# Issuing all loads, bit copies and stores from SyncE's queue, with the whole instruction order laid anew, in a bucketed-attention and MLP kernel

## The chip, the cores and the metric

The kernel runs on one core of a Trainium2 chip. The metric is the device time of one execution in microseconds (us); lower is better. The time before is the median of three runs.

## The reference, cut to what matters

Batch B = 4, H = 8 heads, S = 768 positions, D = 64; the MLP has 512 channels and 2048 hidden units. Each query and key gets six sign bits from a projection; a query attends only to keys whose six bits are all the same as its own.

```python
q_bits = (np.einsum('bhsd,dk->bhsk', q, proj) > 0)
k_bits = (np.einsum('bhsd,dk->bhsk', k, proj) > 0)
mask   = q_bucket[:, :, :, None] == k_bucket[:, :, None, :]   # buckets: the bits as a number
scores = np.where(mask, 0.125 * q @ k.T, -1e9)
attn   = softmax(scores)                                      # sum + 1e-9 below
x      = (attn @ v), the heads side by side: [4, 768, 512]
xn     = (x - mean) / sqrt(var + 1e-6) * g_ln
out    = x + relu(xn @ w_ch1) @ w_ch2
```

## The kernel before, in words

**The order.** The program is a list of 1138 words (ORDER, lines 19 to 117), and the loop at line 561 turns each word into the instructions of one small function. A word reads `name.engine.arguments`; the engine letter is v (VectorE, DVE), a (ScalarE, ACT), p (GpSimd, POOL), s (SyncE, SP) or t (TensorE, PE). Every engine executes its own words strictly in the order of the list, and so does the queue from which it issues DMAs: a DMA word that has to wait holds back everything behind it on its engine. The order and the engine letters were found by annealing against a planner's costs. The semaphores and waits are put in by the framework. It gives each DMA that SP or ACT issues one of eight shared semaphores (99, 101, 103, 105, 106, 107, 108 and 110 in the trace), in turn over both queues together, and a DMA waits, before it is issued, until the last DMA on the same semaphore has landed, whichever queue that one came from.

**The attention.** The work is cut into 12 units u, each 256 queries of one batch (batch b has units 3b to 3b+2), times two groups g of four heads, times three blocks kp of 256 keys: 72 score blocks s = 6u + 3g + kp.

- `LX` (line 393; `lx`, 289, in pieces for batch 0) loads q or k of one batch and head group, 768 KB, into one of four X buffers; `tu` and `tn` turn it in 32 by 32 squares on DVE; `CA` and `ca` (`cast`, 247 to 253) cast it to bf16.
- `hm` (403; `hc` for batch 0) projects it, and `bt` (416) turns the signs into bits. `mo` (419) copies these bits, 4.5 KB at a time, to the partitions where the score matmuls read them, the tile G. That is 16 small SBUF to SBUF DMAs for each batch and head group, 96 in all: the arguments of `mo.b.g.c.i` are batch, group, key quarter c (192 columns) and head i.
- `lv` (354) loads v into one of two buffers, `cv` (360) casts it and `su` (366 to 373, three adds) sums it, both on POOL; `sp` and `sc` spread that sum.
- `S` (432, matmuls at 444) makes a score block from the bits and from q and k, `E` (449) is its exponential on ACT, two halves for each block, `A` (452, 459) multiplies by v and adds up in PSUM.

**The MLP.** `na` (470), `nb` (476; the multiply of 481 reads two SBUF operands), `nc` (483) and `ce` (487; 489 reads two SBUF tensors) divide by the row sum and normalize on DVE, and `rs` (493) makes the inverse deviation on POOL. `fl` (497) transposes xn by a DMA, which only SP issues. `F` (511, matmuls at 516) is a pair of hidden tiles, and `R` (521) its relu, on DVE (526) or ACT (524). F has a single PSUM buffer, f1, so the next F waits for the last R. `D` (528, 532) is a quarter of the second product, `Z` (539) adds the residual on DVE, `O` (545) stores 128 KB of x, which is one of four x buffers.

SP issues 155 DMAs before the change: 7 lx, 15 lv, 10 LX, 71 mo, 22 fl, 30 O. ACT issues 66: the projection, 11 lv, 2 LX, the load of g_ln (`lg`), 25 mo, 26 O. POOL issues the 8 weight loads. ACT's DMA words stand between its exponentials and relus; line 42 of the list begins with `mo.a.1.0.2.1`, and line 68 with `lv.a.3.4.0`.

Of the kernel before, what the change touches and what calls it, by code (L numbers as in the profile page):

```python
# [19 lines left out]
lp.a mem.v p32.p warm.t lx.s.0.0.0.1 tn.v.0.0.0 hc.t.0.0.0 ca.v.0.0.0 bc.v.0.0.0 lx.s.0.1.1.3 tn.v.0.1.2 sel.p  # L20
sl.t.0.0.0 bi.a.0.0.0 on.p.0 hc.t.0.1.2 lx.s.1.0.0.1 bc.v.0.1.2 ca.p.0.1.2 pmem.p sl.t.0.1.2 tn.v.0.1.1 hc.t.0.1.1
tn.v.1.0.0 lx.s.0.1.0.1 bc.v.0.1.1 lx.s.1.1.0.3 ca.p.0.1.1 lv.a.0.0.4 bi.a.0.1.2 S.t.2.2 lx.s.0.0.1.3 tn.v.0.1.0
E.a.2.0 hc.t.1.0.0 lv.s.0.4.4 sl.t.0.1.1 bc.v.1.0.0 sl.t.1.0.0 bi.v.1.0.0 bi.a.0.1.1 tn.v.1.1.1 ca.p.0.1.0 ca.p.1.1.1
hc.t.0.1.0 E.a.2.1 S.t.1.2 bc.v.0.1.0 sl.t.0.1.0 lw1.p.1 tn.v.1.1.0 bi.v.0.1.0 lw1.p.3 hc.t.1.1.0 bc.v.1.1.0
ca.v.1.0.0 hc.t.1.1.1 bc.v.1.1.1 E.a.1.0 cv.p.0.0.0 S.t.0.2 E.a.1.1 E.a.0.0 tn.v.1.1.2 ca.p.1.1.2 cv.p.0.0.2
lx.s.1.0.1.3 E.a.0.1 sl.t.1.1.0 bi.v.1.1.0 sl.t.1.1.1 bi.v.1.1.1 LX.s.1.0.1 hc.t.1.1.2 S.t.4.2 tn.v.0.0.2 E.a.4.0
E.a.4.1 tn.v.0.0.1 hc.t.0.0.1 A.t.0.2 bc.v.1.1.2 lv.s.1.0.0 ca.v.1.1.0 sl.t.1.1.2 bi.a.1.1.2 S.t.3.2 ca.p.0.0.1
tn.v.1.0.2 A.t.1.2 bc.v.0.0.1 cv.p.0.4.0 A.t.2.2 E.a.3.0 tn.v.1.0.1 ca.v.1.0.1 E.a.3.1 sl.t.0.0.1 bi.v.0.0.1
tu.v.1.0.1.2 lg.a sq.t.0.0 sc.a.0.0 S.t.5.2 tu.v.1.0.1.1 E.a.5.0 E.a.5.1 na.v.0.0 hc.t.1.0.2 bc.v.1.0.2 lw1.p.2
ca.v.0.0.2 lw2.p.0 cv.p.0.4.2 sq.t.0.4 sc.a.0.4 lw1.p.0 sl.t.1.0.2 tu.v.1.0.1.0 S.t.8.2 E.a.8.0 E.a.8.1 hc.t.1.0.1  # L30
lv.a.1.0.3 bc.v.1.0.1 A.t.5.2 sl.t.1.0.1 nb.v.0.0 A.t.4.2 A.t.3.2 bi.v.1.0.2 tu.v.1.0.1.3 S.t.6.2 E.a.6.0 na.v.0.1
bi.v.1.0.1 E.a.6.1 hc.t.0.0.2 nc.v.0.0 bc.v.0.0.2 sl.t.0.0.2 LX.s.1.0.0 bi.a.0.0.2 tu.v.1.0.0.3 S.t.7.2 lv.s.1.0.1
nb.v.0.1 nc.v.0.1 E.a.7.0 E.a.7.1 A.t.6.2 A.t.8.2 ce.v.0.0 ft.t.0.0 ce.v.0.1 ft.t.0.1 S.t.9.2 E.a.9.0 E.a.9.1
fc.v.0.1 A.t.7.2 fc.v.0.0 F.t.0.6 R.v.0.6 F.t.0.7 R.a.0.7 S.t.10.2 na.v.1.0 tu.v.1.0.0.0 rs.p.0 F.t.0.2 E.a.10.0
F.t.0.5 lv.s.1.4.0 E.a.10.1 LX.a.1.1.0 R.a.0.2 A.t.9.2 R.v.0.5 tu.v.1.0.0.1 S.t.11.2 E.a.11.0 A.t.10.2 F.t.0.3
tu.v.1.0.0.2 CA.v.1.0.0 F.t.0.4 E.a.11.1 nb.v.1.0 R.a.0.4 S.t.14.2 A.t.11.2 E.a.14.0 R.v.0.3 E.a.14.1 lw2.p.1 F.t.0.0
R.a.0.0 F.t.0.1 lv.s.1.0.2 S.t.12.2 nc.v.1.0 hm.t.1.0 R.a.0.1 na.v.1.1 nb.v.1.1 nc.v.1.1 ce.v.1.0 LX.s.1.1.1 on.p.1
fl.s.1.0 E.a.12.0 ce.v.1.1 bt.v.1.0 D.t.0.0.0 lv.s.1.4.1 fl.s.1.1 E.a.12.1 ca.v.1.0.2 lw2.p.2 S.t.13.2 CA.v.1.0.1
mo.s.1.0.2.0 tu.v.1.1.0.1 tu.v.1.1.1.1 mo.s.1.0.1.3 tu.v.1.1.0.2 tu.v.1.1.0.3 tu.v.1.1.1.0 su.p.1.0 D.t.0.0.1
D.t.0.0.2 tu.v.1.1.0.0 LX.s.2.0.0 E.a.13.0 mo.s.1.0.2.2 A.t.12.2 E.a.13.1 A.t.13.2 S.t.16.2 tu.v.1.1.1.2 tu.v.1.1.1.3  # L40
hm.t.1.1 CA.v.1.1.1 bt.v.1.1 lw2.p.3 lv.s.1.4.2 mo.s.1.0.3.3 D.t.0.0.3 mo.s.1.1.3.3 mo.s.1.0.3.2 lv.a.1.4.3
mo.a.1.0.2.1 Z.v.0.0 E.a.16.1 mo.s.1.0.1.2 F.t.1.2 E.a.16.0 su.p.1.4 A.t.14.2 na.v.2.0 mo.s.1.0.0.1 rs.p.1
mo.a.1.0.0.0 mo.a.1.1.1.0 mo.s.1.1.0.0 S.t.15.2 tu.v.2.0.0.0 R.a.1.2 F.t.1.0 LX.s.2.1.0 D.t.0.1.0 mo.s.1.0.0.3
mo.a.1.1.2.0 cv.p.1.4.0 mo.s.1.0.1.0 tu.v.2.0.0.2 cv.p.1.4.2 mo.s.1.0.3.0 E.a.15.1 mo.s.1.0.2.3 D.t.0.1.1 E.a.15.0
mo.a.1.0.1.1 R.v.1.0 F.t.1.1 S.t.17.2 mo.a.1.0.0.2 nb.v.2.0 nc.v.2.0 R.a.1.1 D.t.0.1.2 F.t.1.5 mo.s.1.1.1.1 E.a.17.0
mo.s.1.0.3.1 R.v.1.5 LX.s.2.0.1 D.t.0.1.3 E.a.17.1 cv.p.1.0.0 mo.s.1.1.0.3 S.t.18.2 E.a.18.0 F.t.1.4 CA.v.1.1.0
A.t.15.2 mo.s.1.1.1.3 Z.v.0.1 R.v.1.4 lv.a.2.0.2 A.t.17.2 A.t.16.2 na.v.2.1 F.t.1.3 lv.s.2.0.1 tu.v.2.0.0.1 E.a.18.1
cv.p.1.0.2 O.s.0.1 lv.a.2.4.3 S.t.20.2 mo.a.1.1.1.2 nb.v.2.1 nc.v.2.1 mo.s.1.1.0.2 ce.v.2.1 D.t.1.0.0 R.a.1.3 F.t.1.6
E.a.20.1 E.a.20.0 D.t.1.0.1 R.v.1.6 S.t.19.2 ce.v.2.0 mo.s.1.1.3.1 mo.a.1.1.0.1 E.a.19.0 F.t.1.7 tu.v.2.0.0.3
D.t.1.0.2 mo.a.1.1.2.1 R.v.1.7 D.t.1.0.3 Z.v.1.0 sp.t.1.0 E.a.19.1 A.t.20.2 sc.a.1.0 S.t.21.2 sp.t.1.4 mo.s.1.1.2.2  # L50
mo.a.1.1.3.2 D.t.1.1.0 E.a.21.0 A.t.18.2 tu.v.2.0.1.0 E.a.21.1 mo.s.1.1.2.3 fl.s.2.1 sc.v.1.4 fl.s.2.0 F.t.2.4
R.v.2.4 rs.p.2 lv.s.2.4.2 S.t.22.2 E.a.22.0 A.t.19.2 E.a.22.1 F.t.2.0 na.v.3.0 tu.v.2.0.1.1 R.a.2.0 D.t.1.1.1
mo.s.1.1.3.0 S.t.23.2 D.t.1.1.2 nb.v.3.0 F.t.2.3 E.a.23.0 E.a.23.1 A.t.22.2 R.v.2.3 LX.s.2.1.1 S.t.24.2 tu.v.2.0.1.2
tu.v.2.0.1.3 hm.t.2.0 E.a.24.1 D.t.1.1.3 E.a.24.0 CA.v.2.0.1 bt.v.2.0 Z.v.1.1 CA.v.2.0.0 tu.v.2.1.1.1 lv.s.2.0.0
nc.v.3.0 F.t.2.1 tu.v.2.1.0.2 R.a.2.1 S.t.26.2 E.a.26.1 F.t.2.5 R.a.2.5 A.t.23.2 A.t.21.2 na.v.3.1 nb.v.3.1 nc.v.3.1
E.a.26.0 F.t.2.6 R.a.2.6 S.t.25.2 E.a.25.1 A.t.26.2 F.t.2.2 ce.v.3.0 E.a.25.0 D.t.2.0.0 mo.a.2.0.2.0 S.t.29.2 on.p.2
lv.s.2.4.1 lv.s.2.0.3 O.s.0.3 R.v.2.2 E.a.29.0 D.t.2.0.1 F.t.2.7 LX.s.3.0.1 O.a.1.1 ce.v.3.1 E.a.29.1 R.v.2.7
D.t.2.0.2 D.t.2.0.3 tu.v.2.1.1.2 fl.s.3.1 Z.v.2.0 S.t.28.2 tu.v.2.1.0.3 rs.p.3 A.t.24.2 mo.a.2.0.1.0 E.a.28.0
su.p.2.0 sp.t.2.0 D.t.2.1.0 O.s.1.3 tu.v.2.1.0.1 cv.p.2.0.0 D.t.2.1.1 E.a.28.1 sc.a.2.0 S.t.31.2 E.a.31.0 fl.s.3.0
F.t.3.2 tu.v.2.1.1.3 D.t.2.1.2 tu.v.2.1.0.0 E.a.31.1 A.t.25.2 R.a.3.2 S.t.27.2 O.s.0.2 CA.p.2.1.0 tu.v.2.1.1.0  # L60
E.a.27.0 na.v.4.0 cv.p.2.0.2 E.a.27.1 mo.a.2.0.2.3 mo.s.2.0.0.1 D.t.2.1.3 mo.s.2.0.0.3 O.s.0.0 nb.v.4.0 mo.s.2.0.1.3
F.t.3.7 Z.v.2.1 O.s.2.2 mo.s.2.0.1.2 R.v.3.7 A.t.29.2 CA.v.2.1.1 S.t.30.2 E.a.30.1 E.a.30.0 F.t.3.6 R.v.3.6 nc.v.4.0
mo.s.2.0.1.1 A.t.27.2 O.a.1.0 lv.a.2.4.0 su.p.2.4 A.t.28.2 na.v.4.1 hm.t.2.1 mo.s.2.0.0.0 LX.s.3.0.0 mo.a.2.0.2.2
S.t.32.2 bt.v.2.1 mo.s.2.1.0.2 nb.v.4.1 E.a.32.0 F.t.3.0 R.a.3.0 A.t.30.2 cv.p.2.4.2 A.t.31.2 F.t.3.1 E.a.32.1
nc.v.4.1 ce.v.4.0 ce.v.4.1 S.t.35.2 A.t.32.2 O.s.2.3 mo.s.2.0.3.2 R.v.3.1 F.t.3.3 R.v.3.3 D.t.3.0.0 mo.s.2.0.3.1
O.a.2.0 mo.s.2.0.2.1 tu.v.3.0.0.2 O.s.2.1 lv.a.3.4.2 fl.s.4.1 E.a.35.0 E.a.35.1 tu.v.3.0.0.3 mo.a.2.1.1.1 S.t.34.2
cv.p.2.4.0 na.v.5.0 LX.a.3.1.1 fl.s.4.0 mo.s.2.1.1.3 F.t.3.4 R.v.3.4 D.t.3.0.1 nb.v.5.0 E.a.34.0 mo.s.2.0.0.2
lv.a.3.4.0 E.a.34.1 A.t.35.2 tu.v.3.0.1.1 tu.v.3.0.1.2 F.t.3.5 R.a.3.5 S.t.33.2 E.a.33.0 E.a.33.1 D.t.3.0.2 F.t.4.0
mo.s.2.0.3.0 D.t.3.0.3 mo.s.2.1.2.0 R.v.4.0 S.t.37.2 Z.v.3.0 F.t.4.5 R.v.4.5 mo.s.2.1.2.2 mo.a.2.1.3.1 LX.s.3.1.0
mo.a.2.1.0.3 E.a.37.1 nc.v.5.0 mo.s.2.0.3.3 A.t.33.2 mo.s.2.1.3.2 tu.v.3.0.0.1 A.t.34.2 E.a.37.0 F.t.4.1 R.v.4.1  # L70
S.t.38.2 D.t.3.1.0 F.t.4.4 E.a.38.0 na.v.5.1 mo.s.2.1.0.1 R.v.4.4 mo.s.2.1.3.3 A.t.37.2 E.a.38.1 S.t.36.2 E.a.36.0
E.a.36.1 nb.v.5.1 F.t.4.2 R.a.4.2 D.t.3.1.1 nc.v.5.1 mo.s.2.1.2.1 mo.s.2.1.2.3 A.t.38.2 mo.s.2.1.1.2 mo.s.2.1.0.0
ce.v.5.1 mo.s.2.1.1.0 lv.a.3.0.1 S.t.39.2 A.t.36.2 F.t.4.7 E.a.39.0 D.t.3.1.2 ce.v.5.0 fl.s.5.0 E.a.39.1 na.v.6.0
lv.a.3.0.2 S.t.40.2 tu.v.3.0.1.3 R.a.4.7 O.s.1.2 D.t.3.1.3 mo.s.2.1.3.0 fl.s.5.1 tu.v.3.0.1.0 CA.v.3.0.1 E.a.40.0
Z.v.3.1 O.s.3.2 F.t.4.3 R.v.4.3 A.t.39.2 E.a.40.1 lv.s.3.4.3 S.t.41.2 D.t.4.0.0 E.a.41.1 tu.v.3.0.0.0 hm.t.3.0
E.a.41.0 bt.v.3.0 mo.s.3.0.1.2 S.t.44.2 E.a.44.0 E.a.44.1 rs.p.4 F.t.4.6 R.v.4.6 O.s.3.3 A.t.40.2 D.t.4.0.1
tu.v.3.1.0.1 lv.a.3.4.1 sp.t.2.4 sc.v.2.4 O.a.3.1 S.t.43.2 CA.v.3.0.0 nb.v.6.0 E.a.43.0 mo.s.3.0.0.0 A.t.41.2
tu.v.3.1.1.3 na.v.6.1 F.t.5.3 cv.p.3.4.2 R.a.5.3 mo.s.3.0.0.2 tu.v.3.1.0.0 D.t.4.0.2 D.t.4.0.3 mo.a.3.0.3.0
# [516 lines left out]
```

## Time and profile before

| | us |
|---|---|
| median of three runs | 323.37 (322.46 to 324.5) |
| the profiled execution's own time | 320.4 |
| its span | 318.7 |
| PE busy | 296.5 |
| DVE busy | 187.2 |
| ACT busy | 178.6 |
| POOL busy | 71.8 |
| mean granted TensorE clock | 0.957 |

The profile is of one execution. Busy is the time in which an engine had an instruction in it, and issuing a DMA does not count as busy. The granted clock (PEclk) is the share of its full clock that TensorE was given. In the trace "ACTq" and "SPq" are the queues from which ACT and SP issue, and a line there with "DMA" is the issue alone; where a DMA landed is read from the semaphore that it updates. In a chain of waits a DMA stands with the time from its issue to its landing.

### The profile page before, as it was taken

The page shows a single profiled execution, that of the slowest core. Times are in us where ns is not written, and L with a number is a line of the kernel's source. Part 1 is how long each engine was busy: PE and PEld are TensorE (multiplying, and loading weights), DVE is VectorE, ACT ScalarE, POOL GpSimd, SP SyncE. Part 2 cuts the span into 40 slices and gives each one's busy share as a digit, 9 for nine tenths or more (in the row PEclk, how much of TensorE's full clock was granted, in tenths as well). Part 3 has the DMA queues.
Part 4 walks back from the last instruction along what each step waited for, and adds up shares of the span by engine and source line. Part 5 has one row for each costly group of instructions (what it writes and reads, how often), then busy time and mean ns, then how long its engine had stood idle before and what let it go on. Part 6 is the DMA issues. An engine that isn't in the chain of part 4 may idle for free.

```text
span 318.7 us, 10198 instructions
## 1 busy us (share of the span) xinstructions
PE 296.5 (93%) x4494; PEld 208.3 (65%) x4538; DVE 187.2 (59%) x373; ACT 178.6 (56%) x194; POOL 71.8 (23%) x95
## 2 busy tenths in 40 slices
PE   6999899879999999759999999999999999999993
PEld 5567686547667668536766676666766776776562
DVE  4666869745738658725749635737544665462222
ACT  2567688436676676444776664566656766532100
POOL 4682350072200572500003050270100101010000
PEclk9559799979999999989999999999999999999999
DMA  7999995736390316370323120121220111103233
GB/s 225 371 268 277 239 216 110 190 110 194 70 281 6 68 39 174 102 226 5 74 75 101 36 60 23 37 56 23 51 66 2 37 35 34 34 2 72 63 82 84
DMA packets 30429, 33.62 MB, mean 105 GB/s; under 512 B 15536, under 2 KB 27056, under 8 KB 30384
## 3 DMA queue, kind: packets, MB, share of 16 engines
q1 hardware_dynamic: 21982, 21.18, 23.1%
q10 hardware_dynamic: 4178, 7.59, 8.7%
q0 software_dynamic: 4224, 4.19, 8.2%
q8 instruction: 35, 0.57, 0.7%
q14 instruction: 10, 0.08, 0.1%
HBM read 27.53 MB, written 6.29 MB: 106 GB/s over the span
## 4 chain that ended last, share of the span: by engine, by line
PE 82%; DMA 5%; DVE 4%; SPq 2%; ACT 2%; issue 2%; ACTq 0%
PE f L516 25%; PE sc L444 17%; PE acc L459 11%; ACT E L450 2%; DMA X<-in_q_dram 2%; PE hp L408 2%; PE hf L314 2%; DMA X<-in_k_dram 1%; DMA G<-B 1%; PE f_01None L532 1%; SPq L420 1%; PE f_101None L532 1%; PE f_91None L532 1%; PE f_41None L532 1%; PE f_100None L532 1%
## 5 line engine op out<-in xcount | busy, mean ns | idle before, releaser
L450 ACT ACTIVATE E<-sc,bias_sb 128x1024 bf16<-128x1024 f32 x144 | 153.3, 1110 | 80.2 <-PE sc L444 68.1
L516 PE MATMUL f<-xnT,w_sb 128*128 128x256 bf16 x768 | 100.5, 275 | 3.2 <-ACT hb L524 1.6
L516 PEld LDWEIGHTS <-w_sb 128*128 128x128 bf16 x768 | 72.0, 98 | 25.4 <-issue 9.1
L526 DVE TENSOR_SCALAR hb<-f 128x512 bf16<-128x512 f32 x57 | 39.3, 690 | 63.7 <-PE f L516 63.1
L532 PEld LDWEIGHTS <-hb 128*128 128x128 bf16 x400 | 37.0, 99 | 34.8 <-issue 7.5
L444 PE MATMUL sc<-qb,kb 32*128 32x256 bf16 x1152 | 55.9, 279 | 0.0
L444 PE MATMUL sc<-G 6*128 6x256 bf16 x576 | 44.0, 282 | 6.0 <-ACT E L450 5.9
L459 PEld LDWEIGHTS <-E 128*128 128x128 bf16 x1152 | 43.4, 100 | 7.2 <-issue 3.7
L524 ACT ACTIVATE hb<-f 128x512 bf16<-128x512 f32 x39 | 23.1, 596 | 42.9 <-PE f L516 41.0
L459 PE MATMUL acc<-vaug,E 128*128 128x65 bf16 x1152 | 46.8, 197 | 0.0
L494 POOL TENSOR_SCALAR rs<-mv 128x2 f32<-128x2 f32 x12 | 7.4, 619 | 125.3 <-DVE mv L488 125.0
L444 PEld LDWEIGHTS <-kb 32*128 32x128 bf16 x1152 | 31.6, 96 | 2.2
L444 PEld LDWEIGHTS <-G 6*128 6x128 bf16 x576 | 16.0, 93 | 23.9 <-issue 21.6
L361 POOL CAST vaug<-vn 128x768 bf16<-128x768 f32 x16 | 14.6, 928 | 53.0 <-DMA vn<-in_v_dram 38.1
L242 DVE STREAM_TRANSPOSE T<-X 128x384 f32<-128x384 f32 x48 | 25.3, 556 | 1.7 <-DMA X<-in_q_dram 1.7
L472 DVE SCALAR_TENSOR_TENSOR y<-vsB,acc 128x520 f32<-128x520 f32 x24 | 16.5, 686 | 16.6 <-PE acc L459 16.6
L489 DVE SCALAR_TENSOR_TENSOR xc<-x,mv,gB 128x512 bf16<-128x512 f32 x24 | 18.6, 776 | 1.0 <-DVE mv L488 0.2
L481 DVE TENSOR_TENSOR x<-y,rc 128x512 f32<-128x512 f32 x24 | 18.5, 773 | 0.8
L485 DVE BATCH_NORM_STATS2 st<-x 128x6 f32<-128x256 f32 x48 | 17.5, 414 | 0.3
L369 POOL TENSOR_TENSOR t<-vn 128x768 f32<-128x768 f32 x6 | 11.2, 1862 | 27.1 <-DMA vn<-in_v_dram 20.9
L242 DVE STREAM_TRANSPOSE tp<-X 128x256 f32<-128x256 f32 x24 | 9.1, 418 | 5.9 <-DMA X<-in_q_dram 4.6
L495 POOL TENSOR_TENSOR rs<-rs,mhalf 128x2 f32<-128x2 f32 x12 | 9.0, 753 | 1.0
(97 smaller groups left out, 225.8 us busy)
## 6 DMA issues: line engine op xcount, KB each, us to landing
X<-in_k_dram SPq DMA_DIRECT2D x6, 768.0 KB
w_sb<-in_moe_w_ch_dram POOLq DMA_DIRECT2D x8, 512.0 KB, 13.3
X<-in_q_dram SPq DMA_DIRECT2D x5, 768.0 KB
out_dram<-x SPq DMA_DIRECT2D x24, 128.0 KB
vn<-in_v_dram SPq DMA_DIRECT2D x14, 192.0 KB
out_dram<-x ACTq DMA_DIRECT2D x20, 128.0 KB
vn<-in_v_dram ACTq DMA_DIRECT2D x10, 192.0 KB
G<-B SPq DMA_DIRECT2D x71, 4.5 KB
```

The costliest lines, as they stand in the source:

```text
L242: nc.vector.transpose(d[:, j], s[:, j, kj0 : kj0 + n])
L444: nc.tensor.matmul(sc(s, i // 2)[:, i % 2, 256 * kk : 256 * kk + 256], lh, rh, start=(rep == 0), stop=(rep == 2), skip_group_check=True,)
L450: nc.scalar.activation(E(s)[:, heads(h)], sc(s, h), AF.Exp, scale=EXP_SCALE, bias=bias_sb)
L459: nc.tensor.matmul(acc[:, qt, (D + 1) * i : (D + 1) * (i + 1)], E(s)[:, i, 256 * kk + P * qt : 256 * kk + P * qt + P], vaug(u // 3)[:, 4 * ...
L472: nc.vector.scalar_tensor_tensor(yt(u, g), vs, EPS_ROW, made[f"acc{u}{g}"][:, :, :A], op0=AOP.mult, op1=AOP.add,)
L481: nc.vector.tensor_tensor(xo, a[:, :, :, 0:D], rc.to_broadcast([P, 2, 4, D]), op=AOP.mult)
L485: nc.vector.bn_stats(stats(u)[:, qt, g], xt(u)[:, qt, 256 * g : 256 * g + 256])
L489: nc.vector.scalar_tensor_tensor(xc(u)[:, t], xt(u)[:, t], mv(u)[:, t, 0:1], gB, op0=AOP.subtract, op1=AOP.mult,)
L516: nc.tensor.matmul(f1[:, n].rearrange("p (t x) -> p t x", t=2), w1_sb[:, dt, P * nt : P * nt + P], xnT(u)[:, :, dt], start=(dt == 0), stop ...
L524: nc.scalar.activation(hb(u)[:, 2 * p : 2 * p + 2], f1, AF.Relu)
L526: eng.tensor_scalar_max(hb(u)[:, 2 * p : 2 * p + 2], f1, 0.0)
L532: nc.tensor.matmul(f2, hb(u)[:, nt, P * t : P * t + P], w2_sb[:, nt, half(h)], start=(nt == 0), stop=(nt == NNT - 1),)
```

## The change

Only the list changes; it was annealed anew with the eight shared semaphores in the planner's model. The same 1138 words stand in a new order, and some have another engine letter:

| words | before | after |
|---|---|---|
| mo (bit copies) | 71 SP, 25 ACT | 96 SP |
| lv, LX, lg (loads) | 25 SP, 14 ACT | 39 SP |
| O (stores) | 30 SP, 26 ACT | 50 SP, 6 ACT (all in the last unit) |
| fl, lx | 22, 7 SP | the same |
| R (relu) | 57 DVE, 39 ACT | 39 DVE, 57 ACT |
| CA (cast of a whole q or k tile) | 11 DVE, 1 POOL | 4 DVE, 7 POOL (4 of q, 3 of k), 1 ACT |
| ca (cast of a piece, batch 0) | 6 DVE, 6 POOL | 1 DVE, 8 POOL, 3 ACT |
| sc | 4 DVE, 4 ACT | 5 DVE, 3 ACT |

SP then issues 214 DMAs, ACT 7. Of the first words on SP, the order before is q of group 0, k of group 0 (512 KB), q of group 1; after, it is q of group 1, q of group 0, k of group 0. The diff replaces all of the list; these are the lines that matter below.

```diff
-lp.a mem.v p32.p warm.t lx.s.0.0.0.1 tn.v.0.0.0 hc.t.0.0.0 ca.v.0.0.0 bc.v.0.0.0 lx.s.0.1.1.3 tn.v.0.1.2 sel.p
...
-fl.s.1.0 E.a.12.0 ce.v.1.1 bt.v.1.0 D.t.0.0.0 lv.s.1.4.1 fl.s.1.1 E.a.12.1 ca.v.1.0.2 lw2.p.2 S.t.13.2 CA.v.1.0.1
...
-D.t.0.0.2 tu.v.1.1.0.0 LX.s.2.0.0 E.a.13.0 mo.s.1.0.2.2 A.t.12.2 E.a.13.1 A.t.13.2 S.t.16.2 tu.v.1.1.1.2 tu.v.1.1.1.3
...
-mo.a.1.0.2.1 Z.v.0.0 E.a.16.1 mo.s.1.0.1.2 F.t.1.2 E.a.16.0 su.p.1.4 A.t.14.2 na.v.2.0 mo.s.1.0.0.1 rs.p.1
-mo.a.1.0.0.0 mo.a.1.1.1.0 mo.s.1.1.0.0 S.t.15.2 tu.v.2.0.0.0 R.a.1.2 F.t.1.0 LX.s.2.1.0 D.t.0.1.0 mo.s.1.0.0.3
...
-lv.a.3.4.0 E.a.34.1 A.t.35.2 tu.v.3.0.1.1 tu.v.3.0.1.2 F.t.3.5 R.a.3.5 S.t.33.2 E.a.33.0 E.a.33.1 D.t.3.0.2 F.t.4.0
...
+lp.a mem.v sel.p p32.p warm.t lx.s.1.0.0.1 tn.v.1.0.0 hc.t.1.0.0 bc.v.1.0.0 lx.s.0.0.0.1 ca.p.1.0.0 sl.t.1.0.0
+tn.v.0.0.0 bi.a.1.0.0 hc.t.0.0.0 lx.s.0.1.1.3 lx.s.0.1.0.1 tn.v.0.1.2 hc.t.0.1.2 bc.v.0.0.0 lx.s.1.1.0.3 lv.s.0.0.4
...
+tu.v.1.1.1.2 A.t.12.2 D.t.0.0.0 D.t.0.0.1 ce.v.1.1 fl.s.1.0 lw2.p.3 rs.p.1 tu.v.1.1.1.0 CA.p.1.1.1 E.a.13.1 S.t.16.2
+E.a.16.0 tu.v.1.1.0.3 fl.s.1.1 mo.s.1.0.2.0 E.a.16.1 lv.s.1.4.0 tu.v.1.1.0.1 hm.t.1.1 lv.s.1.4.2 D.t.0.0.2
+mo.s.1.0.1.1 cv.p.1.0.0 S.t.15.2 bt.v.1.1 A.t.13.2 na.v.2.0 nb.v.2.0 mo.s.1.0.3.3 F.t.1.1 LX.s.2.1.0 E.a.15.0
+E.a.15.1 mo.s.1.0.0.3 mo.s.1.1.1.2 R.v.1.1 mo.s.1.0.3.0 D.t.0.0.3 S.t.17.2 F.t.1.5 R.a.1.5 E.a.17.0 CA.p.1.1.0
+Z.v.0.0 LX.s.2.0.1 su.p.1.0 D.t.0.1.0 cv.p.1.4.0 D.t.0.1.1 F.t.1.0 mo.s.1.0.0.1 nc.v.2.0 E.a.17.1 A.t.15.2 A.t.17.2
+mo.s.1.0.1.2 LX.s.2.0.0 R.a.1.0 su.p.1.4 F.t.1.2 R.v.1.2 lv.s.2.4.3 A.t.16.2 na.v.2.1 cv.p.1.4.2 mo.s.1.1.3.3
+nb.v.2.1 nc.v.2.1 mo.s.1.1.1.3 S.t.18.2 mo.s.1.1.1.0 F.t.1.4 E.a.18.0 mo.s.1.1.1.1 D.t.0.1.2 D.t.0.1.3 R.a.1.4
+E.a.18.1 F.t.1.6 mo.s.1.0.2.1 R.a.1.6 mo.s.1.1.3.2 S.t.20.2 E.a.20.0 mo.s.1.1.0.0 mo.s.1.1.0.3 ce.v.2.1 mo.s.1.1.2.0
...
+sc.a.1.4 mo.s.1.1.2.3 tu.v.2.0.0.3 E.a.19.0 LX.s.2.1.1 D.t.1.0.1 tu.v.2.0.1.1 mo.s.1.1.3.0 E.a.19.1 F.t.1.7 D.t.1.0.2
...
+tu.v.2.1.0.0 mo.s.2.0.0.1 A.t.20.2 su.p.2.4 sp.t.1.0 sc.v.1.0 D.t.1.1.0 D.t.1.1.1 tu.v.2.1.1.0 LX.s.3.0.1 F.t.2.3
...
+D.t.11.1.3.1 Z.v.11.1.1 O.s.11.1.1.1 O.a.11.1.2.1 O.s.11.1.0.1 O.a.11.1.3.1
```

## The prediction

> **What bounds the kernel now.** I read the page first, then a table of windows cut where PE's row dips, then PE's and ACT's timelines in the dips, then the chain of waits there.
>
> ```profile
> PE 296.5 (93%) x4494; PEld 208.3 (65%) x4538; DVE 187.2 (59%) x373; ACT 178.6 (56%) x194; POOL 71.8 (23%) x95
> PE   6999899879999999759999999999999999999993
> PEclk9559799979999999989999999999999999999999
> ```
>
> PE is the bound; no other engine is above 59%. It is short of full at the start, in slices 17 and 18, and at the end. The windows (length; busy us and instructions of PE, PEld, DVE, ACT, POOL; granted clock; DMA share; GB/s) say how much:
>
> ```profile
> 8.00:25.00 17.00, 16.08 (x306) 10.88 (x299) 10.76 (x33) 10.93 (x13) 12.92 (x15) 0.50 1.11 319
> 25.00:41.00 16.00, 14.03 (x313) 11.15 (x311) 11.05 (x29) 11.11 (x14) 4.45 (x8) 0.89 1.08 245
> 61.00:70.00 9.00, 5.73 (x63) 3.92 (x63) 4.16 (x8) 4.83 (x5) 4.33 (x5) 0.81 0.37 107
> 70.00:129.00 59.00, 58.21 (x965) 40.95 (x972) 39.50 (x73) 38.80 (x42) 19.44 (x21) 1.00 0.44 125
> 129.00:145.00 16.00, 10.75 (x127) 6.98 (x126) 6.89 (x13) 6.95 (x7) 3.29 (x4) 0.89 0.52 153
> 145.00:307.00 162.00, 159.81 (x2260) 111.25 (x2289) 92.43 (x172) 89.52 (x96) 20.49 (x26) 1.00 0.18 44
> ...
> 65.98:69.39 3.41, 2.82 (x11) 1.67 (x12) 1.10 (x3) 2.44 (x3) 3.08 (x5) 0.50 0.18 39
> 141.07:144.48 3.41, 3.08 (x23) 1.55 (x17) 0.00 (x0) 2.14 (x3) 0.00 (x0) 0.50 0.26 56
> ```
>
> From 70 to 129 and from 145 to 307 PE is 99% busy at full clock: nothing is to be had there. The losses in the middle are in 61 to 70 and 129 to 145, and the last two rows are stretches at half clock in these. PE's timeline names the idle time before a matmul and what ended it:
>
> ```profile
> 63.89 0.29 PE L444 MATMUL sc<-G 6*128 6x256 bf16 x4 [1.43 <-ACT E L450]
> 66.35 1.86 PE L516 MATMUL f<-xnT,w_sb 128*128 128x256 bf16 x8 [1.62 <-ACT hb L524]
> 131.31 0.38 PE L516 MATMUL f<-xnT,w_sb 128*128 128x256 bf16 x2 [1.61 <-DVE hb L526]
> 140.65 0.28 PE L444 MATMUL sc<-G 6*128 6x256 bf16 x2 [3.25 <-ACT E L450]
> ```
>
> Three of the four waits are for ACT. Its own timeline shows ACT idle with work ready, right behind a DMA of its own queue, until another DMA lands:
>
> ```profile
> 64.91 0.75 ACTq L420 DMA_DIRECT2D G<-B  x1
> 65.70 0.60 ACT L524 ACTIVATE hb<-f 128x512 bf16<-128x512 f32 x1 [1.86 <-DMA X<-in_q_dram]
> 139.10 0.34 ACTq L358 DMA_DIRECT2D vn<-in_v_dram  x1
> 139.49 1.11 ACT L450 ACTIVATE E<-sc,bias_sb 128x1024 bf16<-128x1024 f32 x1 [3.48 <-DMA G<-B]
> ```
>
> The relu does not read X, nor the exponential that bit copy: the DMA word ahead of each waits for a shared semaphore. The chain of waits has both waits:
>
> ```profile
> 58.64 6.19 DMA X<-in_q_dram
> 134.93 4.15 DMA G<-B
> ```
>
> The bit copy at 64.91 waited for SP's 768 KB load, the v load at 139.10 for a bit copy of SP.
>
> **What goes away.** The four idles are 1.43 + 1.62 + 1.61 + 3.25 = 7.9. Behind them come the two stretches of 3.41 us at half clock; PE's 2.82 and 3.08 of work there would have taken half at full clock, so they cost 1.4 + 1.5 = 2.9. Another 0.3 of idle behind the last makes 11.1. After the change ACT issues the projection and six stores of the last unit, so 9.5 of this (all but the DVE idle of 1.61) has no place left to happen. Were some other wait hidden behind it, the word behind would show it: the score block at 140.65 waits for a PSUM buffer alone, and the transposes that F of unit 4 needs landed by 134.4.
>
> The 1.61 is another thing. DVE was late: its multiply L481 took 2.00 against 0.69, and two L489 took 1.01 and 1.07 against 0.75, a sum of 1.88, each while POOL ran an add or a cast. In the new order those words meet other POOL work, so I count the 1.61 as gone and price new meetings below.
>
> **SP.** 25 mo, 20 O, 11 lv, 2 LX and lg come over. By their rows (mo 0.72 on SP, O 0.42, lv 0.42, LX 0.44 at most) this is 18.0 + 14.3 = 32.3 more issue time, on about 106 now (71 x 0.72 + 22 fl x 1.22 + 62 others at about 0.45). 138 of 310 is no bound as a sum. It is one where bit copies come in a heap. All waits for the shared semaphores now run down one queue: a DMA waits for the one eight places ahead, and eight issues of 0.42 to 0.77 are 3.4 to 6.2 us, against landings (from the semaphore events) of 1.8 to 2.1 for a bit copy, 2.2 for a store, 2.4 for a transpose, 4.5 to 7.0 for a 768 KB load. Bit copies right behind such a load land after 3.7 to 4.7. So waits stay short except behind loads.
>
> The tight place is batch 1's copies, S.18 to S.23. I count PE's work from S.8 by its rows (S 0.77, A 0.49, F 0.87, D 0.86, hm 1.44): S.18 starts at 36.5, S.20 at 40.8, S.21 at 47.3, S.23 at 55.2. On SP, `lv.s.2.4.3` stands before the last copies that S.20 needs, and waits for a v buffer, that is for `su.p.1.0`. POOL gets there so: `ce.v.1.1` at 24.0 on DVE, rs 1.4, the k cast CA.p.1.1.1 (no row; 1.6 by L361's cast of 768 columns in 0.82, 3.2 by L253's of 512 in 1.07), cv 0.9, the q cast CA.p.1.1.0 4.11 (L251), su 1.86 + 0.73 + 0.73 = 3.3. That is 35.3 to 36.9. Then lv 0.4 and four copies at 0.77: `mo.s.1.0.2.1` is issued at 38.8 to 40.4 and lands at 40.7 to 42.3. S.20 waits 0 to 1.5; I take 0.7, the middle. Behind it the loads LX.2.0.0 and LX.2.1.1 land 4.5 to 7.0 after their issue, and DVE's `tu` stand ahead of Z and R words that PE needs: 0 to 1.0 and 0 to 1.6; I take 0.3 and 0.6, as the 4.5 is the commoner. S.38's copy stands behind LX.3.1.0: 0 to 0.5, taken 0.2. Sum 1.8, ends 0 and 4.6. In batch 2 (S.36) and batch 3 (S.54 to S.59) the same count leaves 2 us or more.
>
> **ACT, DVE, POOL.** ACT gets 18 relus at 0.596, 10.7, and casts of some 3; DVE loses 18 x 0.69 + 7 x 0.95 = 19. Both stay near 60% under PE's work. If ACT's cover were gone, each relu would cost the path 0.6. POOL gets six casts more, 17 to 22 us. They may meet DVE's two-input words L481 and L489. The rows: 5 of 48 were slowed, by 0.24 to 1.31, and one heap cost PE 1.61. The nearest value to the new load is one such heap: 1.6. Ends: 0, as DVE is idle 41%, and 4.1, the length of the longest POOL cast, once in full.
>
> [...] No row here has a two-input word beside such a cast.
>
> **The start.** The words and bytes up to S.14 are nearly the same (PE work 33.9 against 34.2). The first k piece goes third, not second: one issue (0.65) and 256 KB later (0.7 at 371 GB/s), but that stretch is at 319 GB/s and half clock anyway. I take 0; ends -2 (one 3.41 stretch at half clock fewer) and +3 (that 1.3, and one stretch more). g_ln now stands behind `lv.s.1.0.1`; the first such v load was issued at 19.6 before, so g_ln at about 20.4, and 7.6 to its landing as before gives 28, against a reader (`ce.v.0.0`) at about 33. The tail has its four last stores on two queues in both orders: 0.
>
> **Sum.** -11.1 + 1.8 + 1.6 = -7.7. The profiled execution would go from 320.4 to 312.7; the median was 3.0 above it, so 323.4 - 7.7 = 315.6, say 315.5.
>
> **Rivals.** *Nothing new:* the waits go and no new one comes: 323.4 - 11.1 = 312, or 310 with the good start. For it: 99% busy wherever ACT issues little. Against: no slack at S.20. *SP takes over:* the upper ends, 4.6, with one half-clock stretch (1.7) and the late first piece (1.3): 11.1 - 7.6, so 320. For it: 22 copies in SP's queue from S.14 to S.20, against 17 before. *The waits move:* the change does not do what it says, since ACT's waits were for landings that PE needs soon anyway: 323. Against: the two words it waited for do not feed what it held. *Slower, GpSimd's casts stop DVE:* the four q casts of 4.11 each hold a two-input DVE word that stands ahead of an R or Z: 16.4, with no other gain lost: 323.4 - 11.1 + 16.4 = 328.5. It decides from 11.1 us, nearly three of the four in full. [...]
>
> **How the numbers follow.** This kernel's measurement tells about 1% from no change: 320.1 to 326.6. Nothing new 0.15; the forecast (312.5 to 319) 0.50; SP takes over (319 to 323) 0.18; waits move 0.07; slower 0.10. Faster: 0.15 + 0.50 + 0.06 of the third = 0.71; same 0.12 + 0.07 = 0.19; slower 0.10. The range leaves out the slower case and the waits that move: 309.5 (all gone, good start) to 323.0.
>
> **What would show it.** In the profile after: no ACT idle ended by a DMA; 129 to 145 at full clock; S.20's and S.23's matmuls with idle ended by a bit copy or DVE, under 2 us together; `lv.s.2.4.3` on SP waiting for POOL; L481 and L489 slowed beside POOL's casts. I am wrong if PE stays at 99% through S.24 (then 312), if PE's idle in batch 1 passes 6 us, or if the start moves by more than 3 us.

## The result, and the profile after

The changed kernel takes 311.09 us (median of four runs, 310.78 to 313.1), the kernel before 323.11 beside it (322.46 to 324.5): a ratio of 0.964 with a 95% interval of 0.958 to 0.969. Measured once more, it is 0.974 (0.968 to 0.981), 311.37 against 321.32; there single runs of the kernel before lay between 317.5 and 326.4, those of the changed one between 310.4 and 313.1. Ratios here leave out disturbed runs, so they can stand some tenths of a per cent off two medians. The profiled execution took 311.2 by itself, with a span of 309.5. The page after:

```profile
PE 296.3 (96%) x4538; PEld 205.2 (66%) x4538; DVE 169.6 (55%) x344; ACT 190.5 (62%) x215; POOL 88.7 (29%) x103
PE   6799788999999999999999999999999999999994
PEclk9558999999999999999999999999999999999999
```

PE is as busy as before (296.3 against 296.5) in a span that is 9.2 shorter. The dips in slices 17 and 18 are gone. The windows of before, taken from after (length; busy us and instructions of PE, PEld, DVE, ACT, POOL; clock; DMA share; GB/s):

```profile
61.00:70.00 9.00, 8.78 (x122) 5.43 (x115) 4.45 (x8) 5.75 (x7) 8.84 (x6) 1.00 0.81 259
70.00:129.00 59.00, 58.73 (x968) 41.06 (x965) 39.63 (x74) 41.35 (x45) 22.50 (x26) 1.00 0.38 107
129.00:145.00 16.00, 16.00 (x256) 11.29 (x253) 10.14 (x21) 11.01 (x13) 0.00 (x0) 1.00 0.66 160
145.00:307.00 162.00, 160.19 (x2190) 108.62 (x2182) 77.53 (x143) 92.53 (x107) 28.00 (x28) 1.00 0.21 50
```

The reader is to see PE's 8.78 of 9 and 16.00 of 16, where it had 5.73 and 10.75, and a clock of 1.00 in both. What ACT waited for, from the waits (us in total, times, longest):

```profile
ACT E L450 <- PE sc L444: 64.4, 64, 3.5
ACT hb L524 <- PE f L516: 36.1, 30, 3.1
ACT L337 <- DVE Bc L245: 5.7, 1, 5.7
```

No line of ACT names a DMA any more. PE's longest idle between 61 and 145, where it had idled 1.43 to 3.25 at four places, is now a short one for a DVE relu:

```profile
107.78 1.03 PE L516 MATMUL f<-xnT,w_sb 128*128 128x256 bf16 x8 [0.27 <-DVE hb L526]
```

**A balance by words.** PE's words stand in the trace one behind another. I take the time from the start of one word to the start of the next, less what such a word takes by the rows that the prediction used (S 0.77, A 0.49, F 0.87 and so on), as that word's loss. This counts idle time and half clock together. The sums up to four score blocks are used for all kernels below.

| PE's losses, us | start to S.14 | S.14 to S.23 | S.23 to S.36 | S.36 to S.70 |
|---|---|---|---|---|
| before | 12.7 | 5.8 | 8.6 | 3.6 |
| after | 14.1 | 2.5 | 2.2 | 3.6 |

The middle gives 9.7, the start takes 1.4 back, and the stretch behind PE's last instruction is 0.9 shorter (5.1 to 4.2). That is 9.2, the whole difference of the two profiles. The rest of the 12.0 between the medians is the kernel before itself, whose profiled execution (320.4) was one of its shorter ones.

So the places of the gain are those predicted. Whether the cause is, too, the profile cannot say, because the change does two things at once: it empties ACT's queue, and it moves nearly every word. The first experiments take these apart.

### The profile page after: what moved, and what is told of

It reads as the page before. It is cut to its first block, busy times and chain, and to the rows that moved or that the text cites. A ratio compares the mean times of both kernels' runs of the same rounds, so it can differ in the third digit from the quotient of the medians.

```text
span 309.5 us, 10225 instructions
## 1 busy us (share of the span) xinstructions
PE 296.3 (96%) x4538; PEld 205.2 (66%) x4538; DVE 169.6 (55%) x344; ACT 190.5 (62%) x215; POOL 88.7 (29%) x103
## 4 chain that ended last, share of the span: by engine, by line
PE 89%; DVE 4%; ACT 2%; DMA 2%; issue 1%; SPq 0%
PE f L516 27%; PE sc L444 19%; PE acc L459 12%; PE hp L408 3%; DMA X<-in_k_dram 2%; ACT E L450 2%; PE hf L314 2%; PE f_70None L532 1%; PE f_50None L532 1%; PE f_31None L532 1%; PE f_101None L532 1%; PE f_110None L532 1%; PE f_41None L532 1%; PE f_21None L532 1%; PE f_61None L532 1%; PE f_30None L532 1%
## 5 line engine op out<-in xcount | busy, mean ns | idle before, releaser
L516 PE MATMUL f<-xnT,w_sb 128*128 128x256 bf16 x768 | 99.1, 273 | 1.3 <-issue 0.9
L524 ACT ACTIVATE hb<-f 128x512 bf16<-128x512 f32 x57 | 33.7, 596 | 36.1 <-PE f L516 36.1
L526 DVE TENSOR_SCALAR hb<-f 128x512 bf16<-128x512 f32 x39 | 26.8, 688 | 45.4 <-PE f L516 44.8
L459 PEld LDWEIGHTS <-E 128*128 128x128 bf16 x1152 | 41.8, 99 | 7.0 <-issue 4.3
L459 PE MATMUL acc<-vaug,E 128*128 128x65 bf16 x1152 | 45.5, 195 | 0.0
L494 POOL TENSOR_SCALAR rs<-mv 128x2 f32<-128x2 f32 x12 | 6.3, 528 | 121.3 <-DVE mv L488 120.9
L251 POOL TENSOR_SCALAR qb<-T 128x1536 bf16<-128x1536 f32 x4 | 16.4, 4104 | 25.3 <-DVE T L242 25.3
L489 DVE SCALAR_TENSOR_TENSOR xc<-x,mv,gB 128x512 bf16<-128x512 f32 x24 | 22.0, 917 | 0.8
L361 POOL CAST vaug<-vn 128x768 bf16<-128x768 f32 x16 | 13.1, 829 | 9.9 <-DMA vn<-in_v_dram 9.9
L369 POOL TENSOR_TENSOR t<-vn 128x768 f32<-128x768 f32 x6 | 12.3, 2050 | 8.2 <-DMA vn<-in_v_dram 8.2
```

Source lines behind the costliest of these rows:

```text
L459: nc.tensor.matmul(acc[:, qt, (D + 1) * i : (D + 1) * (i + 1)], E(s)[:, i, 256 * kk + P * qt : 256 * kk + P * qt + P], vaug(u // 3)[:, 4 * ...
L489: nc.vector.scalar_tensor_tensor(xc(u)[:, t], xt(u)[:, t], mv(u)[:, t, 0:1], gB, op0=AOP.subtract, op1=AOP.mult,)
L516: nc.tensor.matmul(f1[:, n].rearrange("p (t x) -> p t x", t=2), w1_sb[:, dt, P * nt : P * nt + P], xnT(u)[:, :, dt], start=(dt == 0), stop ...
L524: nc.scalar.activation(hb(u)[:, 2 * p : 2 * p + 2], f1, AF.Relu)
L526: eng.tensor_scalar_max(hb(u)[:, 2 * p : 2 * p + 2], f1, 0.0)
```

## Experiment 1: the queues alone, the places alone, the letters alone

Four kernels. The first has before's places and only the 59 DMA words moved to SP; the second is after (its places and its computing letters) with the same 59 words given back to ACT; the third and fourth have before's places with after's letters on the computing words, without and with the DMA letters. (The list is wrapped differently in these kernels, so that their line numbers are one or two lower: L442 is 444.)

```diff
-mo.a.1.0.2.1 Z.v.0.0 E.a.16.1 mo.s.1.0.1.2 ...
+mo.s.1.0.2.1 Z.v.0.0 E.a.16.1 mo.s.1.0.1.2 ...
```

> The words in before's places, with before's letters for all computing words; only the 59 loads, bit copies and stores that the change takes from ACT are issued by SP. T1 (the gain is ACT no longer held by its own DMA words, which wait for shared semaphores): 312 to 314, 2% slower than after at most, no idle of ACT ended by a DMA, PE at 99% from 61 to 70 and from 129 to 145 but for the 1.6 that DVE's late word cost. T2 (the gain is the new places and the new letters of the computing words): 321 to 324. T3 (the gain is the issue time that ACT gets rid of, about 25 x 0.75 + 34 x 0.38 = 32 us): 312 to 316 too; the run with six words tells T1 and T3 apart.

> After's places and computing letters, but the same 59 DMA words issued by ACT again. T1: ACT's words wait again for whichever DMA had their semaphore, in new places: 316 to 324, with idle of ACT ended by DMAs that its work does not read, of 4 us or more in sum. T2: 310 to 312, as after. T3: 318 to 324, with ACT issuing but not waiting.

> Before's places and before's queues for all DMAs; only the letters of the computing words are after's (18 relus more on ACT, casts from DVE to POOL, 73 words in all). T1: 322 to 326, the same two waits of ACT near 64 and 139 as before. T2: half of the gain or more, 318 or less.

> Before's places, but all letters of after, DMAs and computing words: only the new places are left out. T1: 311 to 314, as with the DMA letters alone. T2, if the places are what counts: 318 or more.

| | median, us | ratio to before (95%) | to S.14 | to S.23 | to S.36 | to S.70 |
|---|---|---|---|---|---|---|
| DMA letters alone | 320.64 | 0.998 (0.993 to 1.003) | 12.5 | 9.0 | 4.4 | 4.0 |
| after's places, DMAs back on ACT | 319.84 | 0.995 (0.991 to 0.999) | 12.4 | 5.3 | 3.4 | 8.1 |
| computing letters alone | 352.47 | 1.094 (1.076 to 1.113) | 14.7 | 14.7 | 15.0 | 13.0 |
| all letters, before's places | 344.86 | 1.075 (1.062 to 1.087) | 16.1 | 15.2 | 8.7 | 13.0 |

Each theory fails in one of the first two. T1 expected 312 to 314 from the queues alone and got 320.6, though its 316 to 324 for the second came. T2 expected 310 to 312 from the places alone and got 319.8. T3, the 32 us of issuing that ACT gets rid of, expected 312 to 316 of the first and falls with it. By the ratios, neither half is worth more than half a per cent (the intervals leave room for one); both together are worth 3. In the first kernel ACT's waits for DMAs are indeed gone (the words up to S.17 lose nothing), and PE waits a little later:

```profile
72.68 0.37 PE L442 MATMUL sc<-G 6*128 6x256 bf16 x1 [2.54 <-DMA G<-B]
73.77 0.37 PE L442 MATMUL sc<-G 6*128 6x256 bf16 x1 [0.71 <-DMA G<-B]
```

This is S.18, waiting for bit copies. SP's timeline shows why they are late (start, us of issuing, number of DMAs):

```profile
62.94 4.58 SPq L418 DMA_DIRECT2D G<-B  x6
67.56 0.44 SPq L392 DMA_DIRECT2D X<-in_q_dram  x1
68.06 6.88 SPq L418 DMA_DIRECT2D G<-B  x9
74.98 0.44 SPq L392 DMA_DIRECT2D X<-in_k_dram  x1
```

SP issues without a gap, 0.76 for each copy, and the last copy that S.18 reads is issued at 72.69 and lands at 74.50, while PE was there at 70.1. That is the rival *SP takes over*, at the very time it gave, 320. In the second kernel ACT again waits for landings that its exponentials do not read (us in total, times, longest):

```profile
ACT E L448 <- DMA G<-B: 8.3, 4, 2.7
```

After's letters of the computing words cost 7 to 9% in places made for others. T1's 322 to 326 and 311 to 314 miss this, and so does T2's 318 or less; its 318 or more for the fourth holds as a bound alone. The longest loss of the third kernel:

```profile
PE f_00None L530 <- DMA w_sb<-in_moe_w_ch_dram: 8.3, 1, 8.3
```

and POOL's timeline there:

```profile
60.41 1.46 POOL L251 CAST kb<-T 128x1536 bf16<-128x1536 f32 x1 [11.82 <-DVE T L240]
61.81 0.80 POOL L346 DMA_DIRECT2D w_sb<-in_moe_w_ch_dram  x1
```

A cast that DVE did before stands on POOL now, waits 11.82 for its input, and behind it stands the load of the last quarter of w2, issued at 61.81 and not at 43.67 as before.

## Experiment 2: taking single waits away in before's places

If ACT's words held back PE only where the prediction found it, a few of them are enough. One kernel moves six words to SP, those behind which ACT stood idle. One moves no DMA off its queue at all but puts a single X load one place later, so that its semaphore goes next to a copy on SP. One starts from the kernel with the DMA letters alone and puts five issues, which S.18 does not need, behind its last copy.

```diff
-mo.a.1.0.0.0 mo.a.1.1.1.0 mo.s.1.1.0.0 ...
+mo.s.1.0.0.0 mo.s.1.1.1.0 mo.s.1.1.0.0 ...
...
-... LX.s.2.0.0 E.a.13.0 mo.s.1.0.2.2 A.t.12.2 ...
+... E.a.13.0 mo.s.1.0.2.2 LX.s.2.0.0 A.t.12.2 ...
...
-... mo.s.1.0.1.1 ... mo.s.1.0.0.2 ...
+... mo.s.1.0.1.1 ... mo.s.1.0.0.2 mo.s.1.1.3.3 mo.s.1.1.1.0 mo.s.1.1.0.0 LX.s.2.1.0 mo.s.1.1.2.0 ...
```

> Before as it was, but six of ACT's 65 DMA words are issued by SP: the three bit copies around 60 to 65 and the bit copy, the X load and the v load around 133 to 139, behind which ACT stood idle. T1 (ACT held by words that wait; SP must have room for them): the losses at S.15, F.1.0, S.33 and F.4.0 go, 1.5 + 2.3 + 0.6 + 3.8 + 0.4 + 0.9 = 9.5 of PE's time, DVE's 1.6 stays, and SP, which has gaps there in before's trace, takes six issues: 313 to 317. If all that counts is that SP is too full in these places: 319 to 322, as with all 59. T3 (ACT's issue time): six issues of 0.34 to 1.37 are 4 us of 32, so 321 to 323.

> Before, with all DMAs on their queues; one X load on SP (LX.2.0.0) stands behind the bit copy that followed it, one place later. The DMA that gets the load's semaphore next is then a bit copy on SP and not one on ACT. T1: ACT's wait near 64.9 and PE's idle at 63.9 and 66.4 go (about 4.4), the same wait shows on SP (up to 2 us, with room), the wait near 139 stays: 318 to 320.5. If ACT's word waited for something else (the bits, the buffer), nothing moves: 322 to 324.

> As the run with only the 59 DMA words moved to SP, but four bit copies of batch 1's second half and one X load, which S.18 does not read, stand behind the last copy that it reads. If SP's issue time is what S.18 waits for there: the last copy is issued 4 x 0.76 + 0.44 = 3.5 earlier, S.18's wait goes from 3.7 to about 1, and the time is 2 to 3 us under that run's 320.6: 317.5 to 318.5. If S.18 waits for the bits or for a landing behind the load instead: no change, 320 to 321.

| | median, us | ratio to before (95%) | to S.14 | to S.23 | to S.36 | to S.70 |
|---|---|---|---|---|---|---|
| six words | 322.63 | 1.007 (1.001 to 1.013) | 12.9 | 7.4 | 9.6 | 3.6 |
| one load one place later | 323.20 | 1.008 (1.002 to 1.013) | 14.0 | 6.9 | 9.4 | 3.6 |
| five issues later | 322.33 | 1.003 (0.996 to 1.010) | 12.6 | 9.0 | 5.3 | 3.6 |

All three miss the time that was expected if the wait alone held PE back. The first two times lie where the other expectations had put them (T3's 321 to 323, and 322 to 324 for a wait with another cause), but the traces show that neither is the reason, for the waits aimed at do go: with six words moved, S.15 and F.1.0 lose nothing, where they lost 1.5 and 2.3. But PE then loses 3.7 at F.1.6, since ACT now stands behind two other DMA words of its own:

```profile
78.65 0.32 ACTq L357 DMA_DIRECT2D vn<-in_v_dram  x1
79.42 0.77 ACTq L419 DMA_DIRECT2D G<-B  x1
80.23 0.60 ACT L523 ACTIVATE hb<-f 128x512 bf16<-128x512 f32 x1 [5.02 <-DMA vn<-in_v_dram]
```

With the load one place later the wait of 64.9 leaves ACT too. The load lands at 66.72; ACT's copy is issued at 63.27, and SP's copy, which now has the load's semaphore, at 66.74. That shows that the wait belonged to the semaphore's turn and not to the copy or its data. But a relu at 71.58 has waited 3.98 behind the next copies of ACT. With five issues later S.18 waits 0.4, not 3.7 in sum, and what that saves is lost behind it:

```profile
77.28 0.28 PE L443 MATMUL sc<-G 6*128 6x256 bf16 x3 [2.09 <-DMA G<-B]
90.42 1.89 PE L515 MATMUL f<-xnT,w_sb 128*128 128x256 bf16 x8 [3.18 <-DMA xnT<-xc]
```

In before's places the bits, the copies and the loads arrive just about when PE comes by. Whoever frees PE of one wait brings it sooner to the next.

## Experiment 3: an earlier start of the copies

So what do the new places do? The traces answer with one count, the first issue of a bit copy of each batch and group:

| first copy issued at, us | batch 1, g 0 | batch 2, g 0 | batch 2, g 1 | batch 3, g 0 |
|---|---|---|---|---|
| before | 56.1 | 104.7 | 125.4 | 165.7 |
| DMA letters alone | 56.0 | 102.0 | 128.5 | 164.5 |
| after's places, DMAs back on ACT | 47.3 | 87.8 | 113.4 | 150.6 |
| after | 49.0 | 86.8 | 112.2 | 148.2 |

In after's places the copies start 7 to 18 us sooner than before, whichever queue they are on (in batch 3 some 8 of this are PE's own lead by then: S.36 starts at 144.3 and not at 152.5). After's first eight copies on SP:

```profile
48.98 6.36 SPq L420 DMA_DIRECT2D G<-B  x8
```

The next kernel does this for batch 1 alone, on top of the DMA letters.

```diff
-na.v.1.0 tu.v.1.0.0.0 ... tu.v.1.0.0.1 S.t.11.2 ... tu.v.1.0.0.2 ... hm.t.1.0 ... bt.v.1.0 ...
+na.v.1.0 tu.v.1.0.0.0 tu.v.1.0.0.1 tu.v.1.0.0.2 ... hm.t.1.0 bt.v.1.0 S.t.11.2 ...
...
-LX.s.1.1.1 on.p.1 fl.s.1.0 ...
+LX.s.1.1.1 mo.s.1.0.1.3 mo.s.1.0.1.2 mo.s.1.0.0.1 mo.s.1.0.0.0 mo.s.1.0.0.3 mo.s.1.0.1.0 mo.s.1.0.1.1
+mo.s.1.0.0.2 on.p.1 fl.s.1.0 ...
```

> As the run with only the 59 DMA words moved to SP, but batch 1's first bits are made earlier: two transposes on DVE, the hash matmul and the sign words stand ahead of S.11, and the eight bit copies that S.18 reads stand ahead of the transposing loads of unit 1 on SP. Nothing else moves. The first copy of batch 1 would be issued at 46 to 49 instead of 56.0, as after's 49.0. If the new places gain by an earlier start of the copies, with SP's issue time behind it as the limit: eight issues (6.1 us) leave the heap, the 8.4 us that PE lost between 66 and 92 go to under 3, and 320.6 becomes 313 to 316. If the heap only moves (the transposing loads come 6 us later and F of unit 1 waits for them, or the later copies are late all the same): 318 to 321.

It takes 317.03 us, 0.990 (0.986 to 0.994) of before. The DMA letters alone had 0.998 (0.993 to 1.003) on another chip: the two intervals just touch, and the difference of the ratios is some 2.7 us. That is a little short of the expected 313 to 316. Its first copies on SP come at 49.4:

```profile
49.35 6.91 SPq L419 DMA_DIRECT2D G<-B  x8
```

Its losses are 15.0 to S.14, 4.2 to S.23, 5.4 to S.36 and 3.6 to S.70. From S.14 to S.23 that is 4.2 where the DMA letters alone lose 9.0, so the mechanism is shown for that stretch of batch 1. Against the DMA letters alone, 2.5 of this is lost again ahead of S.14 and 1.0 behind S.23; whether the earlier words cost the 2.5 no run tells. Of the 4.2, 1.2 is lost at S.13, where an exponential comes late on a busy ACT, and 1.9 behind a transposing load of unit 2.

What is left of it up to S.36 looked like the DVE word of the prediction, a multiply beside POOL's add and then a relu that PE waits for:

```profile
126.26 2.33 DVE L480 TENSOR_TENSOR x<-y,rc 128x512 f32<-128x512 f32 x1
```

```profile
132.41 1.17 PE L515 MATMUL f<-xnT,w_sb 128*128 128x256 bf16 x8 [1.95 <-DVE hb L525]
```

One more letter, `R.v.3.1` to `R.a.3.1`, gives that relu to ACT:

> As the run with batch 1's copies early, with one letter changed: the relu R.3.1 is done by ACT and not by DVE, where it stood behind the multiply that took 2.33 beside POOL's add (and 0.69 elsewhere). If that meeting is what is left of the middle's losses there: PE's idle of 1.95 before F.3.3 goes, and with it the half-clock stretch behind it (1.2 + 0.6), so 317.0 becomes 313 to 314. If what DVE is late with next (the xc words, R.3.3, the transposes of unit 4) holds PE instead: 316 to 317.5.

318.23 us, 0.984 (0.976 to 0.992) on a chip where before takes 323.36; the interval overlaps the one of 0.990, so this is no gain that can be told. The multiply still takes 2.35, PE no longer waits for that relu, and the time is gone again a few words on:

```profile
137.99 1.05 PE L515 MATMUL f<-xnT,w_sb 128*128 128x256 bf16 x8 [1.44 <-DMA xnT<-xc]
145.38 0.28 PE L443 MATMUL sc<-G 6*128 6x256 bf16 x1 [1.67 <-DMA G<-B]
```

S.38 waits for a copy of batch 2, whose first copy is at 99.7 in the parent kernel and at 86.8 in after. That an earlier batch 2 would close this last gap is what the table suggests; it was not tried by itself.

## Experiment 4: two prices of the prediction, and the start

The seven whole-tile casts of after go back from POOL to DVE; the words ahead of the first score block take before's order; and after runs once more beside them.

```diff
-CA.p.1.1.0 Z.v.0.0 LX.s.2.0.1 su.p.1.0 ...
+CA.v.1.1.0 Z.v.0.0 LX.s.2.0.1 su.p.1.0 ...
...
-lp.a mem.v sel.p p32.p warm.t lx.s.1.0.0.1 tn.v.1.0.0 hc.t.1.0.0 bc.v.1.0.0 lx.s.0.0.0.1 ...
+lp.a mem.v p32.p warm.t lx.s.0.0.0.1 tn.v.0.0.0 hc.t.0.0.0 ca.v.0.0.0 bc.v.0.0.0 lx.s.0.1.1.3 ...
```

> After, with its seven casts of whole q and k tiles on POOL given to DVE (0.95 each), the prediction's price of POOL's casts beside DVE's two-input words taken away. If they cost the path the 1.6 that was counted: 309.5. If they are hidden: 310.6 to 311.6, as after. If DVE's 6.7 us more come at a bad place: 312 to 314.

> After, with the words ahead of its first score block in before's order (first q loads, then the first k piece third) and with before's letters for these computing words. The start of after loses 1.4 us more of PE's time than that of before (to S.14: 14.1 against 12.7). If that is the order of the first pieces: 309.5 to 310. If the words behind expect the other start: 311 to 313.

> The changed kernel once more, on the chip of the three others, as their baseline: 310.8 to 313 as before, with the same place of PE's losses.

Casts on DVE 311.11 (310.75 to 311.55), as expected if the meetings are hidden; sorted start 310.84 (309.07 to 311.91); after 311.37 (310.41 to 313.09): no difference that the runs can tell, so no version is shown to beat after. The meetings themselves are real. In after's trace, DVE's row and then POOL's:

```profile
193.22 2.17 DVE L489 SCALAR_TENSOR_TENSOR xc<-x,mv,gB 128x512 bf16<-128x512 f32 x1
```

```profile
191.62 4.10 POOL L251 TENSOR_SCALAR qb<-T 128x1536 bf16<-128x1536 f32 x1
```

With that cast on DVE the same word, at 192.92, takes 0.75. So the q cast held a two-input word for 1.4, and PE did not notice (from 190 to 200 it was busy 10.00 of 10), as no word that it needed stood close behind.

## Why the prediction came out as it did

The time lies in the range of 309.5 to 323.0, but under the 312.5 to 319 that stood for the forecast's own story: 4.4 under the forecast, and 0.9 under *Nothing new*. The sign of that rival, which the prediction had named as a sign of being wrong, came: from 61 us to S.24 at 95.0 PE is busy 33.80 of 34.02. That the gain came out near the 11.1 that were to go away is in part luck, for the prediction put 9.5 of these on ACT's queue, and the queue alone gave nothing that can be told. Step by step:

- **The 11.1 that go away: right in size for this change, with half of the cause.** All four idles and both half-clock stretches are gone from the middle; against them stand new losses of about 1.4 (0.9 at F.0.3, 0.5 at F.2.7). What failed is the sentence that a wait hidden behind these "would show" in the word behind. I looked only at the very next matmul. Emptying ACT's queue in before's places brings PE to S.18 4.4 before its last copy lands, and no gain is left. The 9.7 needs both halves of the change: no DMA on ACT, and the new places. That what counts in these is copies that start 7 to 18 us sooner is shown for batch 1 and only argued for the rest.
- **SP, +1.8: not there.** No word at S.18, S.20, S.23 or S.38 lost anything. SP's count came near: `mo.s.1.0.2.1` landed at 72.86, 42.5 behind S.8, against 40.7 to 42.3. PE's did not: S.20 came 46.8 behind S.8 and not 40.8. The count had run PE by its rows and left out that the stretch loses time in any case: S.18 came 42.4 behind S.8 and not 36.5, and even before, S.14 came 20.1 behind S.8 for some 16 of work. What was taken for a wait of 0.7 is a slack of 4.2. A count of one engine without its losses, set against another's with them, makes slack look like a wait. That SP's count came near is partly luck, as `lv.s.2.4.3` was not held by POOL: it was issued at 67.46, right behind LX.2.0.0 (66.92 to 67.35), while `su.p.1.0` ran until 67.57.
- **POOL and DVE, +1.6: hidden.** The meetings happen, with 3.4 us more of DVE time in L489 (22.0 against 18.6). A q cast holds one word for 1.4 (2.17 against 0.75), a k cast one for 1.2 (1.94), and five others took 0.4 to 0.8 more beside adds of `su` and casts of v. Taking the seven casts away changes nothing (311.11 against 311.37). No run shows a word held for the 4.11 of a whole q cast, which the upper end of 4.1 counts once and the rival *Slower* four times, as 16.4: by the profile's times, of which POOL's are rough, the word beside the q cast ended at 195.39, before the cast did (195.72), and held until the cast's end it would have taken 2.50 + 0.75 = 3.25. Above all, a held DVE word is not yet a held PE. That rival is out: of its four q casts one met such a word.
- **DVE's 1.61: gone, but no run shows that it was worth 1.61 by itself.** Giving that relu to ACT in the kernel with batch 1's copies early freed no time that can be told.
- **Start 0, tail 0:** 1.4 lost and 0.9 gained in the profiles; the 1.4 is inside the start's bounds, and the tail had none. Sorting the start back gained nothing that the runs can tell.
- **The offset of 3.0 from profile to median: the largest single term that failed.** It was a property of before's runs (317.3 to 327.8 over all of them), whose profiled execution was a short one. After's runs agree within 1% and its profile lies on the median. Without the offset the same sum gives 312.7, against 311.2 for the profiled execution. (Two sums are off by a little: 323.4 - 7.7 is 315.7, and the slower rival's is 328.7.)
- **The rivals.** *SP takes over* did not come, yet it is what the queues alone would have given, 320.6 against 320. *The waits move* described all three kernels of experiment 2.

## What to carry to other kernels

Where one engine is 99% busy between its waits, the transfers behind a wait can be timed to just the lateness that the wait causes, as they were here: before pricing a removed wait in full, move the bound engine up by that much and look at everything that it meets in the next 30 us, not at the next word alone. The bit copies here cost SP their issue time, one behind another (0.76 each, 6.88 for nine), so what helped against a heap was an earlier first issue; reordering the heap did not, and moving DMAs to a queue whose engine computes nothing paid only together with new places. An offset between a profiled run and the median belongs to the kernel that showed it. Letters of engines are not to be carried over without the places they were found with.

## What the runs showed of the hardware that was not expected

Half clock at the start cost almost nothing. From 8 to 25 after has a granted clock of 0.51; the kernel with the sorted start happened to be granted full clock from the first slice on. After's row, then that kernel's:

```profile
8.00:25.00 17.00, 15.02 (x288) 10.10 (x288) 9.91 (x31) 9.22 (x10) 15.23 (x20) 0.51 1.06 307
```

```profile
8.00:25.00 17.00, 15.01 (x300) 10.26 (x300) 10.26 (x33) 9.04 (x10) 14.59 (x20) 1.00 1.08 304
```

PE was busy 15.02 us in after and 15.01 here, and S.8 began at 30.31 and 29.86: 17 us at half clock cost under 0.5. These two start in a different order, but the kernel with the casts on DVE shows the same by itself: three runs with a mean clock of 0.97 took 310.88 to 311.55, and two with 0.997, which leaves no room for such a stretch, 310.75 and 311.11. The likely reason, which no run tests, is that loads set the pace there: the DMA engines are as good as full (share 1.06 and 1.08, at 307 and 304 GB/s).

The length of an idle did not decide whether a half-clock stretch followed. Behind an idle of 1.61 in before (at 131.3) the granted clock was 1.00 up to 134.7, and behind one of 1.92 (one load later, at 82.9) the next F block took 1.03, where the one at half clock in before (at 66.35) took 1.86. Behind 1.95 (copies early, at 132.4) the clock was 0.61 from 132.40 to 135.80 and 0.88 from there to 139.00, in sum 3.4 us at half clock. Nor does the work of PE ahead of these last two tell them apart: in the 3.4 us up to the end of the idle it was busy 44% for the one of 1.92 and 43% for the one of 1.95.

In before's trace the half-clock stretches ahead of the tail last 17.07 us (from 7.95) and three times 3.41 (from 35.26, 65.98 and 141.07). In the 3.41 us ahead of these three PE was busy 2.16, 0.84 and 0.42. Behind 2.28 of 3.41 (before, from 127.42) and 2.50 of 3.41 (after, from 32.35) the clock stayed at 1.00.
